# Decayed attention scores: four 64x64 matmul tiles, one per head and half, in place of two 128x64 tiles with Q laid out block-diagonally

## The chip, the cores and the metric

The kernel runs on one core of a Trainium2 chip. Its engines work from their own instruction queues: TensorE (PE) multiplies matrices, with weight loads (PEld) recorded apart from matmuls; VectorE (DVE) and ScalarE (ACT) do elementwise work; GpSimd (POOL) does a few memsets and issues DMAs; SyncE (SP) issues most DMAs. The metric is device microseconds of one execution, and the time of a kernel is the median of its runs.

## The reference

Two blocks follow each other. The first is a gated linear attention: for each of 4 batches and 8 heads a state of 48x48 is carried over 768 positions.

```
for t in range(S):
    state = alpha[:, :, t, :, None] * state + np.einsum('bhd,bhe->bhde', k[:, :, t], v[:, :, t])
    y[:, :, t] = np.einsum('bhd,bhde->bhe', q[:, :, t], state)
```

Its output, reshaped to x of 3072 x 384, goes through four experts that are mixed by normalised probabilities:

```
for e in range(E):
    h = np.maximum(x @ w1[e], 0.0)          # 384 -> 1024
    out += p[:, e:e + 1] * (h @ w2[e])      # 1024 -> 384
```

All inputs and outputs are float32.

## The kernel before

**Units.** The attention is cut into 24 units: 6 chunks of 128 positions times 4 batches. `attention(u)` (L280) is a generator; each `yield` ends a step. The 24 units are dealt out over the expert work by `deal()`: a list of due times, made from cost estimates in microseconds, says after which expert matmul the next step of which unit is emitted. Within each engine the instructions then run in the order in which they were emitted. The scheduler is manual, so the order is the program's.

**The experts.** `up` (L531) makes the hidden values (matmuls at L570, in the first group L562), `down` (L623, matmuls at L663) brings them back to 384. Most of their matmuls run on float32 values split into three parts. They are the bulk of the work on TensorE.

**One unit.** The heads are padded from 48 to 64 rows, so that a pair of heads fills the 128 partitions. `turned` transposes alpha, K and Q of the unit on TensorE (L277), giving AT, KT and QT as [128 partitions = pair of heads x 64, 4 pairs, 128 positions]. The product of decays between two positions of a chunk is built up in seven levels, with blocks of 1, 2, 4, ... 64 positions. At each level `li`, for the second half of each block, `copy_q` (L321) copies the present Q into a buffer `qb`, `next_q` (L331) multiplies Q by the decay of the first half, and `next_k` (L340) does the same to the keys. So each level has its own Q and its own K, and `products` (L351) multiplies them for that level.

**The scores before.** One weight load holds K of a pair: 128 rows (two heads) by 64 columns (one half `s` of the chunk's positions). If two heads share the 128 rows, a plain Q would add up the scores of both. So `qb` is kept block-diagonal: [128, 4 pairs, 2, 64], where slot `i` of the third axis holds head `i` in its own 64 partitions and zeros in the other 64. The zeros are written once, by four memsets at L778, and `copy_q` fills the two diagonal blocks with two ScalarE copies of 64 partitions (L328). The moving operand for one matmul is then 128 rows by 64 columns (2 heads x 32 positions). The two halves `s` write to partitions 0 to 63 and 64 to 127 of the output, that is to two column tiles of the array. There are 8 matmuls per level, and float32 matmuls are issued as two passes, so a level has 16 recorded matmuls and 16 weight loads.

Levels 0 to 3 are multiplied in one burst, 32 matmuls, into two banks of PSUM named `sc` (levels 0 and 1 in one, 2 and 3 in the other). Level 6, the far scores between the two halves of the chunk (L410), then levels 4 and 5, make a second burst. It uses a bank for `far` and one for levels 4 and 5. The pool has two banks under the tag `sc`.

**After the scores.** `take` (L361) picks the valid scores of a level out of PSUM with a VectorE predicated copy under a mask (L365) into `near`. The far scores go to `lat` by two ScalarE copies (L423), `near` goes to `lat` at L428, and `result` (L436) multiplies `lat` and the carried state by the values (L450, tiles of 32 columns). `turn_keys` and the matmuls at L489 then update the state; seven units use a form of L489 with weight loads of 64 columns in two column tiles.

**The start.** Until the first expert matmul is possible, `fill` (L795) keeps TensorE busy with matmuls on zeros, in numbers written out by hand.

## Time and profile before

| what | value |
|---|---|
| median of 3 runs | 1053.27 us (1052.65 to 1053.30) |
| span of the profiled execution | 1050.8 us, 1.9 to 2.5 us less than the timed runs, which also hold what lies around the span |
| granted TensorE clock | 1.000 over the span |
| busy: PE, PEld | 1033.8 us (98%), 899.2 us (86%) |
| busy: DVE, ACT, POOL | 778.3, 565.7, 37.7 us |
| score matmuls (L355) | 2304 records, 77.2 us busy |
| far matmuls (L410) | 192 records, 15.5 us busy |
| copies of Q (L328) | 336 on ScalarE, 136.6 us busy, 407 ns each |
| predicated copies (L365) | 144 on VectorE, 77.0 us busy |

A group's line gives the source line, the engine, the operation, the tiles written and read, the array tile (rows*columns), the shape of the moving operand, the count, then the busy time in us and the mean duration of one in ns, then the engine's idle time just before and what ended it. Matmuls are pipelined: a duration is longer than the distance from one start to the next, so the cost of a burst is read from starts, not from durations. A line of the timeline gives the start in us from the span's beginning, the time from first start to last end of the merged instructions, and what they are.

### The profile page before, as it was taken

To read this page: it belongs to the slowest core of one execution; us is meant where nothing else is said; L and a number is where in the kernel's file an instruction comes from. 1 tells how busy PE (TensorE), PEld (TensorE's weight loads), DVE (VectorE), ACT (ScalarE), POOL (GpSimd) and SP (SyncE) were. 2 spreads that over 40 slices of the span, in tenths; PEclk is the share of its full clock that TensorE was granted. 3 is DMA by queue.
4 is the path that set the end of the run, shared out by engine and by line. 5 is a ranking of instruction groups with operands and counts; after the bars stand their busy time and mean duration, and the time that the engine had idled before them with its cause. 6 is when DMAs were issued, how large, how long until landed. Compare 5 with 4: busy or idle time off the path is not lost.

```text
span 1050.8 us, 21723 instructions
## 1 busy us (share of the span) xinstructions
PE 1033.8 (98%) x8554; PEld 899.2 (86%) x8554; DVE 778.3 (74%) x1620; ACT 565.7 (54%) x1195; POOL 37.7 (4%) x81
## 2 busy tenths in 40 slices
PE   8899999999999999999999999999999999999998
PEld 8777777687787899898898998898989989898998
DVE  5588777668779868778877777987887875656565
ACT  4687876575657545447456436565474453323232
POOL 3000010000001000000000000000000000000000
PEclk9999999999999999999999999999999999999999
DMA  7596699997868949669669569577594454444531
GB/s 118 161 333 210 241 313 352 320 344 235 300 247 260 382 154 317 270 210 303 241 214 336 187 219 366 183 271 258 170 361 179 183 211 180 182 184 177 207 154 46
DMA packets 158549, 251.66 MB, mean 239 GB/s; under 512 B 120144, under 2 KB 134864, under 8 KB 135920
## 3 DMA queue, kind: packets, MB, share of 16 engines
q1 hardware_dynamic: 151984, 207.89, 58.7%
q0 software_dynamic: 6016, 42.08, 10.0%
q8 instruction: 67, 1.10, 0.4%
q10 hardware_dynamic: 448, 0.32, 0.1%
q14 instruction: 34, 0.28, 0.1%
HBM read 207.79 MB, written 42.47 MB: 238 GB/s over the span
## 4 chain that ended last, share of the span: by engine, by line
PE 85%; DVE 5%; ACT 4%; DMA 2%; issue 2%; SPq 1%; POOL 0%; ACTq 0%; DVEq 0%; POOLq 0%
PE ops L663 36%; PE one L570 23%; PE two L570 11%; PE sc L355 6%; PE yps L450 3%; PE tp L277 3%; ACT qb L328 2%; PE one L562 1%; PE sps L489 1%; DMA hT<-in_moe_w_dram 1%; PE far L410 1%; DVE hT L616 1%; DMA w<-in_moe_w_dram 1%; DVE near L365 1%; DVE QT L335 1%
## 5 line engine op out<-in xcount | busy, mean ns | idle before, releaser
L663 PE MATMUL ops<-w,hT 128*128 128x384 f32 x1872 | 342.7, 340 | 0.2 <-DVE hT L616 0.2
L663 PEld LDWEIGHTS ops<-w,hT 128*128 128x128 f32 x1872 | 322.6, 188 | 4.0 <-ACT t L581 0.6
L570 PE MATMUL one<-xT,w 128*128 128x512 f32 x960 | 251.8, 398 | 0.4 <-ACT t L581 0.4
L570 PEld LDWEIGHTS one<-xT,w 128*128 128x128 f32 x960 | 176.1, 188 | 38.3 <-ACT t L581 1.2
L581 ACT ACTIVATE t<-one 128x512 f32<-128x512 f32 (+1 forms) x192 | 106.7, 556 | 175.1 <-PE one L570 169.9
L328 ACT COPY qb<-QT 64x256 f32<-64x256 f32 x336 | 136.6, 407 | 58.2 <-DVE QT L335 30.3
L610 DVE SCALAR_TENSOR_TENSOR hT<-t,hT 128x512 fp32r<-128x512 f32 (+1 forms) x172 | 110.4, 642 | 63.3 <-ACT hT L608 62.0
L583 DVE TENSOR_TENSOR t<-t,two 128x512 f32<-128x512 f32 (+1 forms) x172 | 109.2, 635 | 53.2 <-PE two L570 32.0
L608 ACT ACTIVATE hT<-t 128x512 fp32r<-128x512 f32 (+1 forms) x172 | 101.8, 592 | 86.8 <-DVE t L583 86.2
L570 PE MATMUL two<-xT,w 128*128 128x512 f32 x480 | 136.5, 393 | 0.1
L570 PEld LDWEIGHTS two<-xT,w 128*128 128x128 f32 x480 | 90.0, 188 | 20.5 <-DVE acc L692 0.9
L663 PE MATMUL ops<-hT 128*128 128x384 f32 x288 | 100.8, 492 | 0.6 <-DMA hT<-in_moe_w_dram 0.3
L616 DVE SCALAR_TENSOR_TENSOR hT<-hT 128x512 fp32r<-128x512 f32 (+1 forms) x172 | 100.6, 634 | 0.0
L365 DVE COPY_PREDICATED near<-masks,sc 128x256 f32<-128x256 uint8 x144 | 77.0, 535 | 22.2 <-PE sc L355 19.3
L335 DVE TENSOR_TENSOR QT<-QT,dec 128x256 f32<-128x256 f32 x144 | 61.0, 423 | 38.8 <-ACT qb L328 38.3
L355 PEld LDWEIGHTS sc<-qb,KT 128*64 128x64 f32 x2304 | 72.7, 138 | 9.0 <-issue 4.4
L355 PE MATMUL sc<-qb,KT 128*64 128x64 f32 x2304 | 77.2, 223 | 2.6 <-ACT qb L328 2.6
L663 PEld LDWEIGHTS ops<-hT 128*128 128x128 f32 x288 | 52.1, 190 | 30.6 <-DMA hT<-in_moe_w_dram 1.2
L692 DVE SCALAR_TENSOR_TENSOR acc<-ops,p_all,acc 128x384 f32<-128x384 f32 x82 | 49.8, 614 | 27.2 <-PE ops L663 26.3
L347 ACT COPY KT<-KT 128x256 f32<-128x256 f32 x138 | 57.5, 417 | 5.1 <-PE sc L355 1.9
L348 DVE TENSOR_TENSOR KT<-KT,dec 128x256 f32<-128x256 f32 x144 | 60.0, 417 | 0.0
L562 PE MATMUL one<-xT,w 128*128 128x256 f32 (+1 forms) x240 | 46.7, 341 | 0.6 <-ACT xT L467 0.6
(90 smaller groups left out, 932.4 us busy)
## 6 DMA issues: line engine op xcount, KB each, us to landing
w<-kept SPq DMA_DIRECT2D x144, 1152.0 KB
kept<-w POOLq DMA_DIRECT2D x32, 1152.0 KB, 7.3
hT<-in_moe_w_dram SPq DMA_DIRECT2D x32, 384.0 KB
w<-in_moe_w_dram SPq DMA_DIRECT2D x48, 128.0 KB
ra<-in_alpha_dram SPq DMA_DIRECT2D x23, 192.0 KB
rk<-in_k_dram SPq DMA_DIRECT2D x23, 192.0 KB
rq<-in_q_dram SPq DMA_DIRECT2D x23, 192.0 KB
out_dram<-acc POOLq DMA_DIRECT2D x22, 192.0 KB, 7.0
```

The costliest lines, as they stand in the source:

```text
L328: nc.scalar.copy(out=qb[rows, :, i, :].rearrange("p a (b r) -> p a b r", r=m), in_=qv[rows])
L335: nc.vector.tensor_mul(qv, qv, spread(dv[:, :, :, 0], m))
L348: nc.vector.tensor_mul(new[:, :, :, 0, :], old[:, :, :, 0, :], spread(halved(decs[li])[:, :, :, 1], m))
L355: nc.tensor.matmul(out[HALF * s:HALF * (s + 1), 2 * p:2 * p + 2, :], lhsT=KTs[li][:, p, HALF * s:HALF * (s + 1)], rhs=qbs[li][:, p, :, QUA ...
L365: nc.vector.copy_predicated(near.rearrange("p a (b two r) -> p a b two r", two=2, r=m)[:, :, :, 1, :], mk.unsqueeze(1).broadcast_to([P, H, ...
L570: nc.tensor.matmul(out, lhsT=w[:, part, kc], rhs=x_part(gi, part, kc), start=(part == terms[0] and kc == 0), stop=(part == terms[-1] and k ...
L581: nc.scalar.activation(out=t, in_=one, func=ACT.Copy, scale=FINE)
L583: nc.vector.tensor_add(t, t, two)
L608: nc.scalar.activation(out=top, in_=x, func=ACT.Relu, scale=TRIM)
L610: nc.vector.scalar_tensor_tensor(out=low, in0=x, scalar=0.0, in1=top.bitcast(F32), op0=ALU.max, op1=ALU.subtract)
L616: nc.vector.scalar_tensor_tensor(out=dif, in0=top.bitcast(F32), scalar=1 / 4096.0, in1=low.bitcast(F32), op0=ALU.mult, op1=ALU.subtract)
L663: nc.tensor.matmul(sums[at], lhsT=h, rhs=w, start=(n == begins[at]), stop=(n == ends[at]))
```

## The change

Q of a level is no longer block-diagonal: `qb` is [128, 4 pairs, 64], filled by one ScalarE copy of all 128 partitions, and its four memsets are gone. Each score matmul takes one head of a pair (64 rows, `i`) and one half of the positions (64 columns, `s`), with a moving operand of 32 columns: four 64x64 tiles of the array, twice as many matmuls, each with half the rows and half the columns. The far scores are cut in the same way, with a moving operand of 64 columns in place of 128.

The outputs of the two heads of a pair go to different banks: one tile `sc` of two banks, [128, 8 heads, 128 columns], with the heads ordered by `i` first and pair second. A level is a stripe of 32 columns in each head, the far scores take columns 64 to 127. The tile has one buffer, so it takes the same two banks as before. `near` and `lat` keep their sizes and take the new order of heads.

```diff
-    blocks = [const.tile([P, NP, 2, HALF], F32, name=f"qb{i}") for i in range(4)]
+    blocks = [const.tile([P, NP, HALF], F32, name=f"qb{i}") for i in range(4)]
...
-            for i in range(2):
-                rows = slice(HD * i, HD * (i + 1))
-                nc.scalar.copy(out=qb[rows, :, i, :].rearrange("p a (b r) -> p a b r", r=m),
-                               in_=qv[rows])
+            nc.scalar.copy(out=qb.rearrange("p a (b r) -> p a b r", r=m), in_=qv)
...
             for p in range(NP):
-                for s in range(2):
-                    nc.tensor.matmul(
-                        out[HALF * s:HALF * (s + 1), 2 * p:2 * p + 2, :],
-                        lhsT=KTs[li][:, p, HALF * s:HALF * (s + 1)],
-                        rhs=qbs[li][:, p, :, QUAD * s:QUAD * (s + 1)], start=True, stop=True)
+                for i in range(2):
+                    rows = slice(HD * i, HD * (i + 1))
+                    for s in range(2):
+                        nc.tensor.matmul(
+                            out[HALF * s:HALF * (s + 1), NP * i + p, :],
+                            lhsT=KTs[li][rows, p, HALF * s:HALF * (s + 1)],
+                            rhs=qbs[li][rows, p, QUAD * s:QUAD * (s + 1)], start=True, stop=True)
...
         def scores():
-            return ps.tile([P, 2, H, QUAD], F32, name="sc", tag="sc")
+            return ps.tile([P, H, P], F32, name="sc", bufs=1)
+
+        level = lambda t, j: t[:, :, QUAD * j:QUAD * (j + 1)]
...
-        banks = [scores() for _ in range(2)]
+        bank = scores()
         for li in range(4):
-            products(li, banks[li // 2][:, li % 2])
+            products(li, level(bank, li))
...
         bank = scores()
-        far = ps.tile([P, NP // 2, 2, HALF], F32, name="far", tag="sc")
+        far = bank[:, :, HALF:]
 
         for r in range(NP // 2):
-            for s in range(2):
-                nc.tensor.matmul(far[HALF * s:HALF * (s + 1), r],
-                                 lhsT=KTs[6][:, 2 * r + s, :HALF], rhs=qbs[6][:, 2 * r + s],
-                                 start=True, stop=True)
+            for i in range(2):
+                rows = slice(HD * i, HD * (i + 1))
+                for s in range(2):
+                    nc.tensor.matmul(far[HALF * s:HALF * (s + 1), NP * i + 2 * r + s, :],
+                                     lhsT=KTs[6][rows, 2 * r + s, :HALF],
+                                     rhs=qbs[6][rows, 2 * r + s], start=True, stop=True)
...
-        parts = lat.rearrange("p (r s i) c -> p r s i c", s=2, i=2)
+        by_half = lambda t: t.rearrange("p (i r s) c -> p s i r c", i=2, s=2)
         for s in range(2):
             rows = slice(HALF * s, HALF * (s + 1))
-            nc.scalar.copy(out=parts[:HALF, :, s, :, HALF:], in_=far[rows])
+            nc.scalar.copy(out=by_half(lat)[:HALF, s, :, :, HALF:], in_=by_half(bank)[rows, s, :, :, HALF:])
...
-                            rhs=QT[:, p, :] if past else lat[:, 2 * p + i, :],
+                            rhs=QT[:, p, :] if past else lat[:, NP * i + p, :],
...
-        for t in values + blocks:
+        for t in values:
             nc.gpsimd.memset(t, 0.0)
```

More of the change, by code (lines that the diff above doesn't have):

```diff
@@ L379, in attention @@
         copy_q(3)
-        nc.vector.tensor_mul(near, ident_all[:, P:].unsqueeze(1).broadcast_to([P, H, HALF]),
-                             dot.unsqueeze(2).broadcast_to([P, H, HALF]))
+        nc.vector.tensor_mul(
+            near.rearrange("p (i a) n -> p i a n", i=2),
+            ident_all[:, P:].unsqueeze(1).unsqueeze(1).broadcast_to([P, 2, NP, HALF]),
+            dot.rearrange("p (a i) -> p i a", i=2).unsqueeze(3).broadcast_to([P, 2, NP, HALF]))
         yield
-        banks = [scores() for _ in range(2)]
+        bank = scores()
         for li in range(4):
-            products(li, banks[li // 2][:, li % 2])
+            products(li, level(bank, li))
         next_q(3)
         next_k(3)
-        take(0, banks[0][:, 0])
-        take(1, banks[0][:, 1])
+        take(0, level(bank, 0))
+        take(1, level(bank, 1))
         yield
@@ L394, in attention @@
         next_k(4)
-        take(2, banks[1][:, 0])
-        take(3, banks[1][:, 1])
+        take(2, level(bank, 2))
+        take(3, level(bank, 3))
         yield
@@ L405, in attention @@
         bank = scores()
-        far = ps.tile([P, NP // 2, 2, HALF], F32, name="far", tag="sc")
+        far = bank[:, :, HALF:]
         for r in range(NP // 2):
-            for s in range(2):
-                nc.tensor.matmul(far[HALF * s:HALF * (s + 1), r],
-                                 lhsT=KTs[6][:, 2 * r + s, :HALF], rhs=qbs[6][:, 2 * r + s],
-                                 start=True, stop=True)
+            for i in range(2):
[4 more added lines that the diff above has]
+                                     rhs=qbs[6][rows, 2 * r + s], start=True, stop=True)
         for li in (4, 5):
-            products(li, bank[:, li - 4])
+            products(li, level(bank, li - 4))
         free.append(qbs[6])
-        take(4, bank[:, 0])
-        take(5, bank[:, 1])
+        take(4, level(bank, 0))
+        take(5, level(bank, 1))
         next_k(6)
         yield
-        parts = lat.rearrange("p (r s i) c -> p r s i c", s=2, i=2)
+        by_half = lambda t: t.rearrange("p (i r s) c -> p s i r c", i=2, s=2)
         for s in range(2):
             rows = slice(HALF * s, HALF * (s + 1))
-            nc.scalar.copy(out=parts[:HALF, :, s, :, HALF:], in_=far[rows])
+            nc.scalar.copy(out=by_half(lat)[:HALF, s, :, :, HALF:], in_=by_half(bank)[rows, s, :, :, HALF:])
         yield
```

## The prediction

> **What bounds the kernel now.** I read the page first: busy times, the chain that ended last, the costliest groups.

> ```profile
> PE 1033.8 (98%) x8554; PEld 899.2 (86%) x8554; DVE 778.3 (74%) x1620; ACT 565.7 (54%) x1195; POOL 37.7 (4%) x81
> ...
> PE 85%; DVE 5%; ACT 4%; DMA 2%; issue 2%; SPq 1%; POOL 0%; ACTq 0%; DVEq 0%; POOLq 0%
> ...
> L328 ACT COPY qb<-QT 64x256 f32<-64x256 f32 x336 | 136.6, 407 | 58.2 <-DVE QT L335 30.3
> ...
> L365 DVE COPY_PREDICATED near<-masks,sc 128x256 f32<-128x256 uint8 x144 | 77.0, 535 | 22.2 <-PE sc L355 19.3
> ...
> L355 PE MATMUL sc<-qb,KT 128*64 128x64 f32 x2304 | 77.2, 223 | 2.6 <-ACT qb L328 2.6
> ...
> L347 ACT COPY KT<-KT 128x256 f32<-128x256 f32 x138 | 57.5, 417 | 5.1 <-PE sc L355 1.9
> ```

> TensorE is the bound, and 85% of the chain lies on it. Hardly anything keeps it waiting: the score matmuls waited 2.6 us in all for copies of Q. So the question is how long the score and far bursts occupy TensorE. A duration does not tell that, since matmuls overlap; starts do. Hence the groups with their shapes kept apart, then the timeline.

> ```profile
> L410 PE MATMUL far<-qb,KT 128*64 128x128 f32 x192 | 15.5, 283 | 2.2 <-DVE t L298 1.3 <-ACT qb L328 0.8
> ...
> L489 PE MATMUL sps<-rv,AT 128*128 128x96 f32 x104 | 13.5, 273 | 0.6 <-ACT AT L475 0.6
> ...
> L489 PE MATMUL sps<-rv,AT 128*64 128x48 f32 x112 | 4.7, 226 | 0.0
> ```

> ```profile
> 23.44 1.08 PE L450 MATMUL yps<-lat,rv 128*32 128x128 f32 x32
> ...
> 511.88 2.09 PE L355 MATMUL sc<-qb,KT 128*64 128x64 f32 x64
> ...
> 513.08 1.50 DVE L365 COPY_PREDICATED near<-masks,sc 128x256 f32<-128x256 uint8 x2 [1.23 <-PE sc L355]
> ...
> 516.34 0.69 DVE L583 TENSOR_TENSOR t<-t,two 128x512 f32<-128x512 f32 x1 [1.24 <-PE two L570]
> ...
> 524.40 0.67 PE L489 MATMUL sps<-rv,AT 128*64 128x48 f32 x16
> ...
> 524.90 0.62 PE L410 MATMUL far<-qb,KT 128*64 128x128 f32 x8
> ...
> 525.36 1.10 PE L355 MATMUL sc<-qb,KT 128*64 128x64 f32 x32
> ...
> 699.14 0.34 PE L663 MATMUL ops<-w,hT 128*128 128x384 f32 x1
> 699.41 0.33 PE L410 MATMUL far<-qb,KT 128*64 128x128 f32 x2
> ```

> Distance of starts = (length - one duration) / (count - 1). Scores: (2090 - 223) / 63 = 29.6 ns. In the first 0.07 us of that burst exactly two matmuls start, 7 ns apart:

> ```profile
> 511.88 0.28 PE L355 MATMUL sc<-qb,KT 128*64 128x64 f32 x2
> ```

> So the two column tiles run side by side, and a round of both takes 59 ns; a level is 8 rounds. What sets 59? The state matmuls with loads of 64 columns move only 48 columns and take (670 - 226) / 15 = 29.6 ns, the same round of 59. Those with 128-column loads and 96 moving columns come in 13 bursts of 8: (13.5 / 13 - 0.273) / 7 = 109 ns. The round follows the columns of the weight load, not the moving columns.

> **The change part by part**, against the span of 1050.8 us; the median of the runs, 1053.27, is 2.5 us more, and I add that at the end.

> *Scores (144 levels).* 16 matmuls and 16 loads a level become 32 and 32. Each of the four tiles still takes 8 loads of 64 columns per level. If the four run side by side, a level stays 8 rounds of 59 ns: nothing gained, because halving the moving columns is no help where the load sets the pace. No run of before puts two heads on different rows, so this is the unknown. Lower bound: 0, by the 48-column row. Upper bound: the two row tiles take turns, 8 x 59 = 0.47 us more a level, x144 = +68 us. I take side by side, since column tiles do it in three shapes, and add 1 ns a round for four staggered starts: (48 + 4) rounds x 24 units = +1.2 us.

> *Issue.* TensorE gets 2304 + 192 more matmul records and as many loads. The quickest sustained pair of load and matmul in the trace is in the values matmuls, (1080 - 273) / 31 = 26 ns; four tiles in 59 ns need 15 ns. If 26 were the limit, the 128 + 64 + 16 = 208 pairs of a unit would take 5.41 us; now six levels take 6 x 0.47 = 2.82 and far 0.46, in all 3.28: +2.1 us, x24 = +51 us. Against that: the 26 ns row has 128 moving columns on four tiles, which may set its pace, and the 7 ns between first starts shows that instructions are ready much faster. I take 0 and keep the 51.

> [...]

> *Far scores (24 units).* Now 0.46 us from the first far to the first score matmul (524.90 to 525.36). After: 16 records, 4 rounds of four. The load is 64 columns as before, the moving operand 64 in place of 128, which is the scores' old shape: 4 x 59 = 0.24, and 0.01 for its start. -0.21 x 24 = -5.0 us. If the row tiles take turns: 8 x 59 = 0.47, no gain.

> *Switching the array.* From an expert matmul to the far burst 0.27 us pass (699.14 to 699.41), where the expert matmuls follow each other at about 0.175: 0.1 us. From the 64-column state matmuls (last start 524.85) to far 0.05: nothing, as both use 128*64. Such state matmuls stand directly before far in 7 units, and now differ: 7 x 0.1 = +0.7 us. Elsewhere there is a switch in both kernels.

> *ScalarE.* 336 copies at 407 ns become 168 at 417 (the K copy of 128x256): 136.6 - 70.1 = 66.5 us less, nearly all off the path. What TensorE waited for copies of Q: 2.6 + 0.8 us. Bounds 0 and -3.4; I take -1.5, since part lies in the first units. At the start the copies in unit 0 shorten, but TensorE runs a fixed number of fill matmuls there and VectorE its own queue: 0, at most -1.

> *VectorE.* Levels 0 to 3 now share one tile. The first `take` waited for levels 0 and 1; in the built order of the changed kernel it waits for the end of level 3, 0.93 us later. Queued behind it are the expert's elementwise steps, for which TensorE waits in the end. It waited for scores 16 times: at most 16 x 0.93 = +15 us. I take 0: at 516.34 VectorE sits idle 1.24 us for TensorE anyway, right after such a wait; if that slack is used up, the split of hidden values is late next. The ScalarE copies of far likewise wait for levels 4 and 5; ScalarE is idle 46% of the time, and what stands behind them are activations: 0.

> *Rest.* Four memsets of qb go (POOL busy 4%): 0. No DMA moves; the added instructions are fetched in 16 KB packets on a queue with a 0.4% share: 0. `near`, `take`, `lat` handle as many elements: 0.

> Sum: -5.0 + 1.2 + 0.7 - 1.5 = -4.6. Some six units lie before 170 us. By the table of stretches TensorE is busy for 126 of the 134 us from 36 to 170, and the chain there holds transfers, so some of their gain is lost: +0.7. Span 1050.8 - 3.9 = 1046.9, runs **1049.4 us**.

> **Rivals.**
> 1. *Row tiles take turns* (slower): +68 on scores, nothing on far, +0.7: about 1121 us. For it: nothing in the trace shows two row tiles at once. Against: column tiles overlap in loads and streams, with two and with four. It decides once a round of four takes over 62 ns: each ns is 1.25 us. [...]
> 2. *Issue sets the pace* (slower): 0 to +51 - 5, so up to 1099; around 1070 if instructions queued ahead carry half a burst.
> 3. *VectorE or ScalarE late after the burst*: up to +15 - 4, so 1050 to 1064. For it: 19.3 us of waits already at L365. Against: 1.24 us idle behind them.
> 4. *More gain than the sum*: the ScalarE relief reaches the path at start and in the late waits, 1041 to 1045.

> **Numbers.** Likeliest case 0.56, its own range 1045 to 1054; rival 1: 0.15, rival 2: 0.15, rival 3: 0.09, rival 4: 0.05. A range of 8 in 10 must reach into rival 2: 1044 to 1080 leaves out rival 1, a fifth of rival 2 and part of 4. A change of 0.2% is 2.1 us, about what a measurement tells from none. Faster (below 1051.2): 0.44 of the likeliest, and rival 4: 0.49. Same: 0.08 and 0.02 of rival 3: 0.10. Slower: the rest, 0.41.

> **What would show it.** Score bursts of 128 records in about 2.1 us with starts 14 to 15 ns apart, four in the first 0.05 us, and far to first score 0.25 us, mean the sum holds. A burst of 4 us with starts 30 ns apart is rival 1; starts near 20 to 26 that drift apart as a burst goes on are rival 2; unchanged bursts with idle time at L570 or L663 behind VectorE are rival 3. I am wrong above all if two heads cannot load or stream at once.

## The result and the profile after

| | before | after |
|---|---|---|
| median | 1052.91 us (1052.16 to 1053.30, 6 runs) | 1062.67 us (1060.18 to 1067.06, 6 runs) |
| ratio | | 1.0094, 95% interval 1.0071 to 1.0117 |
| profiled execution, its span | span 1050.8 us | 1064.29 us, span 1062.5 us |
| granted clock over the span | 1.000 | 0.993 |

The changed kernel is 0.9% slower. The forecast was 1049.4, faster; the time lies inside the range, 1044 to 1080, but on the other side of no change.

The page of the changed kernel: busy times, the instruction queue that grew (packets, MB, share), the shares of the chain, and the groups of the scores and of the copies around them.

```profile
PE 1035.2 (97%) x11050; PEld 900.8 (85%) x11050; DVE 776.9 (73%) x1620; ACT 489.3 (46%) x1027; POOL 36.1 (3%) x77
...
q8 instruction: 87, 1.43, 0.6%
...
PE 92%; DVE 3%; ACT 2%; issue 2%; SPq 1%; DMA 1%; POOL 0%; ACTq 0%; DVEq 0%; POOLq 0%
...
L365 DVE COPY_PREDICATED near<-masks,sc 128x256 f32<-128x256 uint8 x144 | 77.0, 535 | 47.2 <-PE sc L355 44.5
...
L326 ACT COPY qb<-QT 128x256 f32<-128x256 f32 x168 | 68.4, 408 | 74.8 <-DVE QT L332 46.0
...
L355 PE MATMUL sc<-qb,KT 64*64 64x32 f32 x4608 | 77.5, 219 | 8.1 <-issue 7.2
```

There are 2496 more matmuls and as many loads on TensorE, at almost the same busy time. ScalarE is 76 us less busy. New is the entry behind the score matmuls: 7.2 us of idle time that nothing in the profile releases ("issue"); before, their only idle time was 2.6 us behind copies of Q. The instruction queue carries 20 packets more; its line before the change:

```profile
q8 instruction: 67, 1.10, 0.4%
```

4992 more matmuls and loads in 20 packets is 250 each, and 1.43 MB in 87 is 16 KB each: a packet is a block of about 250 instructions. The stops in the table below lie 17, 4, 7, 4, 14 and 3 times 256 instructions apart, so I take 256.

First, what went as forecast. A first burst and a second burst in the timeline (start, length, and what they are), in stretches without such idle time:

```profile
515.47 2.07 PE L355 MATMUL sc<-qb,KT 64*64 64x32 f32 x128
...
527.99 0.67 PE L495 MATMUL sps<-rv,AT 128*64 128x48 f32 x16
528.59 0.46 PE L416 MATMUL sc<-qb,KT 64*64 64x64 f32 x16
528.87 1.09 PE L355 MATMUL sc<-qb,KT 64*64 64x32 f32 x64
```

128 matmuls take 2.07 us where 64 took 2.09: (2070 - 219) / 127 = 14.6 ns from start to start, so four tiles in 58 ns, all side by side. From the first far matmul to the first score matmul 0.28 us pass, before 0.46.

Now what was not forecast. The chain of work in order of time around another first burst (start, length, what):

```profile
554.79 1.67 PE yps L456 x56
556.46 1.51 PE sc L355 x90
557.97 1.90 issue
559.87 0.96 PE sc L355 x38
560.83 2.86 PE one L576 x6
563.69 0.76 PE two L576 x3
```

After 90 of the 128 matmuls TensorE stops for 1.90 us and then goes on with the same burst; its operands were all there, since the other 38 wait for nothing new. And the six expert matmuls behind it take 2.86 us; in quiet stretches six take about 1.5. The table of stretches of the same place (busy time and instructions of PE, PEld, DVE, ACT, POOL; then granted clock, DMA share, GB/s) says why:

```profile
core 0: us, PE busy (x) PEld busy (x) DVE busy (x) ACT busy (x) POOL busy (x), PEclk, DMA share, GB/s
...
555.20:557.70 2.50, 2.50 (x137) 2.30 (x126) 1.16 (x4) 1.18 (x3) 0.00 (x0) 1.00 1.04 431
557.70:559.90 2.20, 0.30 (x18) 0.19 (x10) 0.00 (x0) 0.14 (x1) 0.00 (x0) 1.00 0.54 222
559.90:560.30 0.40, 0.40 (x28) 0.40 (x32) 0.00 (x0) 0.00 (x0) 0.00 (x0) 1.00 0.05 23
560.30:563.70 3.40, 3.40 (x30) 2.76 (x24) 1.98 (x3) 0.00 (x0) 0.00 (x0) 0.50 0.02 5
```

For 3.4 us after the stop the clock is halved, 1.7 us lost. I then went through all starts on TensorE after 40 us and listed the distances above 0.45 us that no wait accounts for. Seven are left; I call them stops. The table is counted from the trace: "position" is the number of TensorE instructions (matmuls, loads and semaphore instructions) recorded before the stop.

| stop at, us | length, us | position | remainder by 256 | time of the 256 before, us | half clock behind it |
|---|---|---|---|---|---|
| 226.66 | 2.28 | 6080 | 192 | 3.19 | 3.41 us |
| 427.49 | 2.14 | 10432 | 192 | 2.46 | 3.41 us |
| 475.78 | 1.34 | 11456 | 192 | 4.39 | none |
| 557.75 | 2.12 | 13248 | 192 | 2.57 | 3.41 us |
| 604.28 | 1.47 | 14272 | 192 | 3.19 | none |
| 760.55 | 1.00 | 17856 | 192 | 2.15 | none |
| 794.57 | 2.86 | 18624 | 192 | 2.46 | 3.41 us |

All seven have the same remainder, so each lies at the edge of a block. They add up to 13.2 us, the halved clock to 4 x 1.7 = 6.8. At all seven a packet of the instruction queue started 2.2 to 2.4 us before the matmuls went on (at 557.69, for one, which took 0.97 us; matmuls at 559.87). What is special at these places is the last column but one. Ahead of the first burst the values matmuls of another unit stand (56 in 1.67 us), and now 128 score matmuls follow: 256 instructions are used up in 2.2 to 4.4 us. Before the change the quickest such block after 40 us took 5.49 us, and no stop lay at an edge. A quick block is not enough, though: after 40 us the changed kernel has thirteen that took less than 4.5 us, and six of them ended without a stop. Ahead of those six edges the packet had started 2.7 to 7.2 us before the matmuls behind the edge.

The account: between the same expert matmuls of the two kernels, the jumps of time at these places come to 18.4 us (a part of the 20.0 falls into waits that stood there before). The span is 11.7 longer, so all the rest of the change gained 6.7 us.

### The profile page after: what moved, and what is told of

Read it like the earlier page. It is cut to its first block, busy times and chain, and to the rows that moved or that the text cites. A ratio compares the mean times of both kernels' runs of the same rounds, so it can differ in the third digit from the quotient of the medians.

```text
span 1062.5 us, 26524 instructions
## 1 busy us (share of the span) xinstructions
PE 1035.2 (97%) x11050; PEld 900.8 (85%) x11050; DVE 776.9 (73%) x1620; ACT 489.3 (46%) x1027; POOL 36.1 (3%) x77
## 3 DMA queue, kind: packets, MB, share of 16 engines
q8 instruction: 87, 1.43, 0.6%
## 4 chain that ended last, share of the span: by engine, by line
PE 92%; DVE 3%; ACT 2%; issue 2%; SPq 1%; DMA 1%; POOL 0%; ACTq 0%; DVEq 0%; POOLq 0%
PE ops L669 38%; PE one L576 24%; PE two L576 12%; PE sc L355 6%; PE tp L277 3%; PE yps L456 3%; PE one L568 2%; PE sps L495 1%; PE idle L801 1%; PE sc L416 1%; SPq L221 1%; DVE near L365 1%; DMA rq<-in_q_dram 1%; DVE w L237 0%; ACT qb L326 0%
## 5 line engine op out<-in xcount | busy, mean ns | idle before, releaser
L576 PE MATMUL one<-xT,w 128*128 128x512 f32 x960 | 255.5, 402 | 1.0 <-issue 0.9
L576 PEld LDWEIGHTS one<-xT,w 128*128 128x128 f32 x960 | 178.7, 191 | 39.1 <-issue 1.5
L365 DVE COPY_PREDICATED near<-masks,sc 128x256 f32<-128x256 uint8 x144 | 77.0, 535 | 47.2 <-PE sc L355 44.5
L326 ACT COPY qb<-QT 128x256 f32<-128x256 f32 x168 | 68.4, 408 | 74.8 <-DVE QT L332 46.0
L355 PE MATMUL sc<-qb,KT 64*64 64x32 f32 x4608 | 77.5, 219 | 8.1 <-issue 7.2
L355 PEld LDWEIGHTS sc<-qb,KT 64*64 64x64 f32 x4608 | 72.8, 135 | 14.8 <-issue 12.1
```

The source lines that it names most:

```text
L326: nc.scalar.copy(out=qb.rearrange("p a (b r) -> p a b r", r=m), in_=qv)
L355: nc.tensor.matmul(out[HALF * s:HALF * (s + 1), NP * i + p, :], lhsT=KTs[li][rows, p, HALF * s:HALF * (s + 1)], rhs=qbs[li][rows, p, QUAD ...
L365: nc.vector.copy_predicated(near.rearrange("p a (b two r) -> p a b two r", two=2, r=m)[:, :, :, 1, :], mk.unsqueeze(1).broadcast_to([P, H, ...
L576: nc.tensor.matmul(out, lhsT=w[:, part, kc], rhs=x_part(gi, part, kc), start=(part == terms[0] and kc == 0), stop=(part == terms[-1] and k ...
```

## The experiments

Three theories. **A:** TensorE runs out of instructions at block edges, because the change packs twice the instructions into the same time just behind another dense stretch. **B:** VectorE, whose first take now waits for the end of level 3 (idle time behind scores 19.3 us, now 44.5), or the shared banks, hold TensorE up. **C:** the 64x64 form itself makes TensorE stop or lose its clock. For B the trace has little: the longest wait of TensorE for VectorE is one of 1.1 us, for `hT`. The waits of TensorE in the changed kernel (total, times, longest):

```profile
PE sc L355 <- issue: 7.2, 4, 2.6
...
PE two L576 <- issue: 1.9, 1, 1.9
PE two L576 <- DVE hT L616: 1.1, 1, 1.1
PE one L576 <- issue: 0.9, 1, 0.9
```

### The first burst split over two steps

The changed kernel, with levels 0 and 1 multiplied one step earlier than levels 2 and 3, so that no 128 score matmuls stand in one piece.

```diff
-        yield
         bank = scores()
-        for li in range(4):
+        for li in range(2):
+            products(li, level(bank, li))
+        yield
+        for li in range(2, 4):
             products(li, level(bank, li))
```

> The changed kernel with its first score burst cut in two: levels 0 and 1 are multiplied one step earlier, levels 2 and 3 stay. Same matmuls, same tiles, same shared banks; the first VectorE take still waits for the end of level 3. Theory A (TensorE runs out of instructions: they come in blocks of 256, and a block that is used up in under about 4.5 us is gone before the next has come): 256 instructions now take longer everywhere, so of the 7 stalls at a block's edge (13.2 us in all) at most two short ones are left, the clock stays at or near 1.000, and the time is the changed kernel's 1062.7 less 13 of stalls less 7 of half clock plus 24 more entries and exits of the tile form at 0.2 us: about 1048 (1045 to 1052). Theory B (VectorE's later take, or the shared banks): nothing is relieved, 1062 plus 5 for the entries. Theory C (the 64x64 form itself stalls or throttles TensorE): the same stalls within bursts, 1062 or more.

Measured: 1052.11 us beside 1052.50 of before, ratio 0.9997 (0.9988 to 1.0006), profiled span 1050.1 at clock 0.999. One stop above 0.45 us is left at a block edge, at 785.61, of 0.46 us. So the loss of 10 us goes with the stops, as A has it, with every 64x64 matmul and both shared banks kept; that speaks against C, and against B too, since the first take still comes behind level 3 (VectorE's idle time behind scores is 28.3 us). The forecast of some 1048 was too low. One burst of 128 takes 2.20 us from the last start before it to the first behind it; two of 64 take 2 x 1.27 = 2.54. Less an expert matmul's own 0.17 to 0.2 us, the second change of the array's form costs about 0.15 us a unit, 24 x 0.15 = 3.6. With the 0.5 of the stop, 4.1 of 6.7 us of gain are accounted for, and the span shows 0.7 of it left; where the other 2 went was not traced.

### The far scores alone

The kernel before, with only the far scores cut into 64x64 tiles, a bank per head; the matmuls of levels 0 to 5 as they were. The two banks are one tile with one buffer, as in the change.

```diff
-            return ps.tile([P, 2, H, QUAD], F32, name="sc", tag="sc")
+            return ps.tile([P, 2, 2, H * QUAD], F32, name="sc", bufs=1)
...
-            for s in range(2):
-                nc.tensor.matmul(far[HALF * s:HALF * (s + 1), r],
-                                 lhsT=KTs[6][:, 2 * r + s, :HALF], rhs=qbs[6][:, 2 * r + s],
-                                 start=True, stop=True)
+            for i in range(2):
+                rows = slice(HD * i, HD * (i + 1))
+                for s in range(2):
+                    nc.tensor.matmul(far[HALF * s:HALF * (s + 1), i, r, :],
+                                     lhsT=KTs[6][rows, 2 * r + s, :HALF],
+                                     rhs=qbs[6][rows, 2 * r + s, i, :], start=True, stop=True)
```

> The kernel before with one part of the change alone: the far scores in four 64x64 tiles, a bank for each head, out of the block-diagonal Q; the scores stay as 8 matmuls of 128 rows a level. The two banks are one tile with one buffer, as in the change, so the first take waits for level 3. Theory A: bursts have half the instructions of the changed kernel, no block is used up in under 5 us, no stall: before less 24 x 0.21 us plus 7 x 0.1: 4 us less than before (2 to 6 less). Theory B: the shared tile makes VectorE late as in the changed kernel: not faster than before, up to 10 us slower. Theory C: 24 short bursts of the form, a quarter of the loss or less: before plus 0 to 3.

Measured: 1055.30 us, ratio 1.0028 (1.0017 to 1.0040), slower than before, though in the profiled execution no stop above 0.45 us lies at a block edge and the clock is 1.000. The timeline of one second burst:

```profile
525.23 0.67 PE L493 MATMUL sps<-rv,AT 128*64 128x48 f32 x16
525.83 0.46 PE L414 MATMUL sc<-qb,KT 64*64 64x64 f32 x16
526.22 1.15 PE L355 MATMUL sc<-qb,KT 128*64 128x64 f32 x32
```

The far burst is as short as in the changed kernel, 0.46 us. But the scores behind it start 0.39 us after its start, not 0.28: the array changes its form inside the burst, 64*64 to 128*64. Far and levels 4 and 5 together take 1.473 us, before 1.518: only 0.045 is gained a unit where the change gains 0.220. In the seven units with state matmuls ahead the burst took 1.484 before, so 0.011 is gained there, and the entry costs 0.1 more: 17 x 0.045 - 7 x 0.09 = 0.1 us of gain in all. At 45 us the trace is 1.5 us behind that of before, where the values of a unit wait for `lat` (4.2 us in all, before 2.8); but at 154 us it is 0.2 ahead, at 182 us 0.6 behind, and its span (1051.9) is 1.1 us longer. How much of that is the shared tile no run separates.

The median lies 1.6 us above the profiled execution's own time, 1053.69. The seven executions fall into two groups by their clock: two at 1.000 took 1053.69 and 1054.31 us, five at 0.997 or 0.998 took 1055.22 to 1056.23. One stretch of 3.41 us at half clock lowers the mean by 0.0016 and costs 1.7 us, so half clock is the likely reason of more than half of the 2.8 us that are lost; none of the five was traced. Here, then, the far tiles were worth little while the burst around them kept the other form.

### As many instructions, in the kernel before

To separate A from C: the kernel before, with 32 needless matmuls (128 more instructions a unit, the number that the change adds to a first burst) ahead of level 0. They have the old kernel's 32-column tiles; their results are overwritten.

```diff
+        for n in range(32):
+            j = n % 4
+            nc.tensor.matmul(banks[0][QUAD * j:QUAD * (j + 1), 0, 0, :], lhsT=KTs[0][:, 0, :QUAD],
+                             rhs=KTs[0][:, 0, :QUAD], start=True, stop=True)
         for li in range(4):
             products(li, banks[li // 2][:, li % 2])
```

> The kernel before, tiles, banks and Q unchanged, with 32 needless matmuls (32 columns loaded, 32 moved, four column tiles) ahead of each first score burst, which then has as many instructions as in the changed kernel. They write into the bank that level 0 overwrites. Work on TensorE: 24 x 64 pairs at about 8 ns = 12 us. Theory A: stalls of 1 to 3 us at the edges of 256-instruction blocks in 4 to 12 of the bursts and some stretches of half clock: 12 plus 10 to 35 us more than before, 1075 to 1100. Theories B and C: only the 12 us, 1063 to 1067, with no stall within bursts and the clock at 1.000.

Measured: 1072.84 us (2 runs), ratio 1.0196 (1.0177 to 1.0215). The chain around one burst:

```profile
431.52 1.67 PE yps L454 x56
433.19 0.59 PE sc L387 x48
433.77 1.43 PE sc L355 x44
435.20 2.86 issue
438.06 0.80 PE sc L355 x19
```

The old form of the scores now stops in the middle of a burst, and it does so at a block edge: six stops (0.9 to 3.1 us, 9.4 us in all) have the remainder 192, behind blocks that took 2.6 to 5.6 us, and at all six the matmuls went on 2.2 to 2.4 us after a packet's start. Nine other blocks as quick ended without a stop above 0.45 us. The form has no part in it; C falls for the stops. But the clock stays at 1.000 here, also behind the stop of 3.08 us, so a stop alone does not bring the halved clock.

### The same needless matmuls, elsewhere

The same 32 matmuls, one step away from the first burst, into a bank of their own that nobody reads. The number of instructions is that of the run above.

```diff
+            if li == 1:
+                other = ps.tile([P, NP, P], F32, name="tp", tag="w")
+                for n in range(32):
+                    j = n % 4
+                    nc.tensor.matmul(other[QUAD * j:QUAD * (j + 1), 0, :QUAD], lhsT=KTs[0][:, 0, :QUAD],
+                                     rhs=KTs[0][:, 0, :QUAD], start=True, stop=True)
             yield
```

> The kernel before with the same 32 needless matmuls per unit as in the dense run, but at another step, the one of level 1, away from the score burst and from the values, among expert matmuls; they write a bank of the transposes. Theory A: the same instructions with slow ones around them use up no block in under 5 us: no stall of over 0.4 us at a block's edge, clock 1.000; 12 us of work and 24 entries and exits of the tile form at 0.2 to 0.3 us: 1069 to 1074. If the needless matmuls themselves stall TensorE: stalls as in the dense run, 1075 or more.

Measured: 1066.44 us (2 runs), ratio 1.0131 (1.0112 to 1.0149). The matmuls themselves cost more here (up to 0.9 us a unit, 0.6 in the run above), which I put down to an entry and an exit of their own. Still the kernel is 6.4 us quicker, and no stop above 0.45 us lies at a block edge; the shortest block after 40 us takes 5.49 us, with 0.23 us behind it. TensorE's waits, first of the run above and then of this one:

```profile
PE sc L355 <- issue: 5.9, 4, 2.9
PE yps L454 <- ACT lat L432: 2.7, 3, 1.4
```

```profile
PE sc L355 <- ACT qb L328: 1.9, 2, 1.2
PE far L416 <- ACT qb L328: 1.2, 1, 1.2
```

The same instructions, fetched in the same 79 packets, cost stops when they stand close together and none when they don't. So it is not the amount of instruction traffic but how closely the instructions stand: with no 256 of them used up faster than in 5.49 us, no stop came.

### The edges moved

The changed kernel with 128 more instructions on TensorE near the start (`pad`, matmuls on zeros, in place of four of the fill matmuls), so that every edge falls 128 instructions earlier in the work.

```diff
-        fill(7)
+        fill(3)
+        pad(36)
```

> The changed kernel with 128 more TensorE instructions at the start, in place of four of the fill matmuls and 36 small ones (about the same length), so that every burst stands half a block later in the instruction stream. Theory A: every stall of over 0.9 us without a semaphore behind it still falls on the same place in the count of TensorE's recorded instructions, 192 past a multiple of 256, but in other bursts: those at 427, 557 and 794 us go, others come (3 to 9 in all). Theories B and C: the same bursts stall as in the changed kernel, now 64 past a multiple of 256. The time tells little: 1052 to 1075.

Measured: 1062.70 us (2 runs), ratio 1.0099 (1.0081 to 1.0118). The burst that ran through in the changed kernel (128 matmuls at 515.47, shown above) now stops:

```profile
515.73 1.83 PE L355 MATMUL sc<-qb,KT 64*64 64x32 f32 x110
520.04 0.48 PE L355 MATMUL sc<-qb,KT 64*64 64x32 f32 x18 [2.48 <-issue]
```

Eight stops, from 0.54 to 2.70 us, again all with the remainder 192, and at other places: all seven of the changed kernel are gone, and the eight are new, at 187.94, 314.24, 517.34 and 828.33 for example. It is the edge that decides which burst stops, and no property of the burst. That the two kernels take the same time says less: the stops merely add up alike, to 12.8 and 13.2 us.

### Only the second burst in 64x64 tiles

The last two are to keep the gain and leave out the dense first burst. First, levels 0 to 3 in the old form, far and levels 4 and 5 in four tiles; Q stays block-diagonal in all buffers, with its two copies.

```diff
-        for li in range(4):
-            products(li, level(bank, li))
+        for li in range(4):
+            products_wide(li, first[li].rearrange("p (i a) q -> p i a q", i=2))
```

> Levels 0 to 3 stay in the old form (128 rows, block-diagonal Q, 8 matmuls a level); levels 4 and 5 and the far scores, the whole second burst, go in four 64x64 tiles, a bank for each head, reading the diagonal blocks of the same Q. Q is copied in two halves as before. The banks are one tile with one buffer. Theory A: the first burst has 128 instructions as before and the second 160, so no block of 256 is used up in under 5 us, and there is no stall and no half clock; the second burst is 0.22 us shorter (no change of the array's form inside it, unlike with far alone): 24 x -0.22 + 7 x 0.1 = -4.6, less what transfers take back before 170 us and what the shared tile costs in the first units: 3 us less than before (1 to 5 less). Theory B (the shared tile and VectorE's later take): no faster than before. Theory C (the form stalls by itself): slower than before.

Measured: 1052.34 us beside 1052.48, ratio 0.9999 (0.9990 to 1.0008). No stop lies at a block edge with more than 0.45 us. The profiled span is 2.2 us shorter than that of before, but that execution, 1050.44 us, is the quickest of eleven; so the expected 3 us are not there in the median. The trace is 0.98 us ahead of that of before at 18 us, 0.95 behind at 45 us and 0.3 ahead again at 154 us; the other 2 us are gained behind that, as the second bursts should. What the median lacks goes with the clock: it was 1.000 in the profiled execution alone, 0.998 in nine others and 0.996 in one, while the sixteen executions of before were at 0.999 or 1.000. A stretch at half clock costs 1.7 us, and the median lies 1.9 us above the profiled execution. That this is the reason is not shown: no execution at 0.998 was traced, and in the split kernel, where seven of ten were at 0.998, the times do not follow the clock.

Then the same, but units 0 to 5, which lie in the stretch where ScalarE and the transfers are late, entirely as in the change, with one plain copy of Q a level.

```diff
+            if u < 6:
+                dirty.add(id(qb))
+                nc.scalar.copy(out=qb[:, :, 0, :].rearrange("p a (b r) -> p a b r", r=m), in_=qv)
+                return
+            if id(qb) in dirty:
+                dirty.remove(id(qb))
+                nc.vector.memset(qb[HD:, :, 0, :], 0.0)
...
+        if u < 6:
+            first = [level(bank, li) for li in range(4)]
+            for li in range(4):
+                products(li, first[li])
+        else:
```

> As the kernel with the second burst alone, but the first 6 units as in the whole change: all levels in four 64x64 tiles and one plain copy of Q for a level (written over one slot of the block-diagonal buffers, whose zeros are restored by a VectorE memset when a later unit takes the buffer). In the first 100 us, where TensorE waits for ScalarE, the changed kernel was 2.7 us ahead of the one before. Theory A: that lead, part of it lost to transfers by 155 us, comes on top: 5 us less than before (3 to 8 less), with at most one stall, in units 2 to 5. If plain copies are worth nothing: as with the second burst alone.

Measured: 1049.24 us beside 1052.48, ratio 0.9970 (0.9959 to 0.9982): 3.2 us quicker than before and 13 quicker than the changed kernel, with no stop above 0.45 us at an edge that a wait does not account for. The second burst is that of the changed kernel, 1.299 us from the first far matmul to the matmul behind it. The clock of the profiled execution is 0.996: two stretches at half clock, from 39.46 and 135.04 us, stand behind waits of TensorE for a copy of Q (1.67 us) and for a transfer (2.26 us). Its dense first bursts in units 0 to 5 met no edge that hurt; that they could not was not shown. The forecast of 5 us was 2 too high.

## Why the prediction was right or wrong

**The step that failed** stands in the paragraph *Rest*: "the added instructions are fetched in 16 KB packets on a queue with a 0.4% share: 0". The queue's share is still only 0.6%, and yet the term is +18.4 us. What counts is not the queue's share but the time until the next block is there: at the seven stops, and at the six of the needless matmuls, the matmuls went on 2.2 to 2.4 us after its packet's start. Time of the block plus the stop behind it is 3.2 to 5.7 us at the seven stops of the changed kernel, and 3.5 to 7.1 at the six of the needless matmuls; behind longer blocks no stop above 0.5 us lay at an edge that a wait does not account for. The numbers for this lay in the trace of before: 67 packets, and a quickest block of 5.49 us. Putting 128 more instructions in the same 2.1 us, right behind 56 dense values matmuls, should have been checked against that. The blocks show in the 20 packets for 4992 instructions and in the one remainder by 256 of all stops; at seven of the thirteen edges behind a block that was used up in less than 4.5 us, 1.0 to 2.9 us were paid.

**Issue, and rival 2.** As a rate the step held: pairs of load and matmul start every 14.6 ns, far below the 26 ns that were its bound, and the starts keep that distance to the end of the burst. Rival 2 gave a price of up to 51 us to the wrong mechanism: the 18.4 us went to the stops at block edges and the halved clock behind four of them, not to the pace between. That the time fell into the range rests on this rival's width, and not on its reason.

**Scores, +1.2.** Side by side was right. The staggered starts cost nothing that can be seen: the first burst takes 17 ns less than before from start to next start (2.20 for 2.22 us), where 1 ns a round, 32 ns a burst, was added. Rival 1 is out: 58 ns a round.

**Far, -5.0, and switching the array, +0.7.** Right to the size. Measured 0.220 less from the first far matmul to the matmul behind the second burst in 17 units. In the seven with state matmuls ahead of it the burst takes 1.299 us for 1.484, and 0.1 is lost again at the entry: 0.085. Together 17 x 0.220 + 7 x 0.085 = 4.3 us, as the two terms gave (5.0 - 0.7).

**ScalarE, -1.5, and the loss to transfers, +0.7.** The mechanism was right and the sizes were low. The trace is 4.4 us ahead of that of before at 127 us, 2.8 at 154: the relief at the start is larger, and so is what the transfers take back. Of the 6.7 us of gain outside the stops 4.3 are the second bursts and 0.4 the first; about 2.0 are left for these two terms, where 0.8 was forecast. Rival 4 thus had something in it, off the stops.

**VectorE, 0, and rival 3.** Right. Its idle time behind the scores rose from 19.3 to 44.5 us, a part of that by the stops themselves, and TensorE waited 1.1 us for `hT`.

So the sum without the stops would have been 6.7 us of gain, against 3.9 forecast; the stops turned it into a loss.

## What to carry to other kernels

When a change cuts matmuls into smaller tiles, look not only at the array: count TensorE's instructions, loads and semaphore instructions included, and find the shortest time in which the kernel uses up 256 of them. Where that fell to 2 to 4.4 us here (once at 5.6), TensorE ran dry at some of the block edges, those where the next packet had started only 2.2 to 2.4 us before the matmuls went on, and a count of instructions that moved by 128 only chose other victims; putting other work between two dense stretches cured it. And cut a whole burst or none of it: the change of the array's form inside a burst cost 0.11 of the 0.18 us that the far tiles gained.
